# Eleven half chunks of second weights held back instead of fourteen, and five token tiles stored by halves of their rows instead of six

## The chip, the cores and the metric

One core of a Trainium2 chip runs the whole program. The metric is device time in microseconds (us) of one execution: the median of the runs before is 177.27 us, from 177.13 to 177.78 in three runs. The execution that the profiler recorded took 176.73 us, and its span, from the first recorded instruction to the last, is 175.0 us. Every time of the form "at 151.5" below counts from the start of that span.

## What is computed

Windowed attention over 8 batches, 8 heads, 576 positions and 64 features per head (one half of the heads with a plain window of 32, the other with a dilated one), then a soft mixture of 8 experts with 4 slots each over all 4608 tokens of 512 features.

```python
attn = softmax(mask(q @ k.T / sqrt(64))) @ v          # per batch and head
x = attn.transpose(0, 2, 1, 3).reshape(4608, 512)
logits = x @ phi                                      # 4608 x 32 slots
d = softmax(logits, axis=tokens)
slot_input = (d.T @ x).reshape(8, 4, 512)
for e in range(8):
    h = relu(slot_input[e] @ w1[e])                   # 512 -> 1024
    slot_out[e] = h @ w2[e]                           # 1024 -> 512
c = softmax(logits, axis=slots)
out = c @ slot_out                                    # 4608 x 512, float32
```

The part that the change touches is the end: the product with the second weights `w2` (8 experts of 1024 x 512), which gives 32 rows of 512, and the last line, which multiplies these 32 rows with every token's weights and stores 9.44 MB of output.

## The kernel before

The kernel is a list of operations with costs and due times. A planner (`Prog.schedule`) puts them in an order for each engine when the program is built, and `Prog.emit` writes that order out with the semaphore waits between engines. GpSimd and SyncE keep the order of the text. While the attention of 8 units runs, GpSimd issues every load: q, k and v of the units, then the first weights w1 of all experts, then the second weights w2. All loads are float32 in memory and become bfloat16 on the way in. They go through one queue, so they land in the order in which they were issued.

The second weights of one expert are 8 chunks (`cc` = 0 to 7), each 128 partitions by 512 columns. The load of an expert is one transfer, or several where `wload` gets a list of parts: (first chunk, last chunk, first column, last column). A piece of one chunk with 256 of its 512 columns is a half chunk here. The last three experts' second weights lie in the buffer `TT` (in the profile `TT<-in_moe_w_dram`, from line 496): w25 whole, then w26 (expert 6) and w27 (expert 7) in six transfers: two whole chunks of w26, the left column halves of its other six chunks, the left halves of w27 in two pieces, then the right halves of w26's six chunks, then the right halves of w27 in two pieces. So fourteen half chunks, all of right halves, come last: these are the ones held back.

The end of the kernel uses this order. `ffn2` multiplies hidden rows with chunks of w2, on four column groups of TensorE at once, into one PSUM bank, `sp_` (line 1017 in the profile). A call with `h_` None works on all 512 columns, with `h_` 0 or 1 on the left or right 256. When the left half of the columns is complete, `half(0, ...)` runs before the rest of the weights has come: VectorE scales the 32 rows into `so_sb` (line 1051), and for each of the first `NAB` token tiles (256 tokens each, two rows of the output to a partition) TensorE multiplies (lines 1069 and 1082), VectorE or ScalarE scales the result by the row sums `rtok` into a buffer in `WD` (lines 1051, 1052 and 1094), and the left halves of the rows are stored at once. Tile 0 is stored in two pieces of 128 KB, the others in one of 256 KB. Stores of even tiles are issued by SyncE (SP), those of odd tiles by ScalarE (ACT) on a queue of its own, both from line 1046. After the rest of the weights, `half(1, ...)` does the same with the right halves. The remaining tokens then go in larger groups (line 1126, tiles of 512 or 1024 tokens with whole rows): two groups of 4 rows to a partition, two of 8, each stored whole by SP, 1 MB, 1 MB, 2 MB and 2 MB.

A stored half row is 256 floats, 1024 bytes in one piece in memory; a whole row tile has 2, 4 or 8 rows in one piece to a partition, so 4, 8 or 16 KB.

Between waits TensorE runs products of a constant buffer (`filler`, line 1144), which the planner puts in where it expects a gap; nothing that they compute is used.

Names for what follows: `wload("w26", ...)` at lines 905 and 907, `NAB` and `GRP` at lines 979 and 980, the list of `ffn2` calls from line 1100, the last loop from line 1112.

Of the kernel before, what the change touches and what calls it, by code (L numbers as in the profile page):

```python
# [57 lines left out]
class Op:  # L58
    n = 0
# [58 lines left out]
class Prog:  # L118
# [6 lines left out]
    def op(self, e, fn, r=(), w=(), a=(), alloc=(), cost=0.5, key=0.0, mode="f",  # L125
           sem=None, nbytes=0, after=(), ndma=1, n=0, port=False):
        o = Op(e, fn, cost, key, mode)
        deps = list(after)
        for b in r:
            deps += b.ready  # L130
        for b in w:
            b.fresh()
            deps += b.prev
        for b in a:
            deps += b.prev
        seen = set()
        for d in deps:
            if d.id not in seen:
                seen.add(d.id)
                o.deps.append(d)  # L140
        for b in r:
            b.reads.append(o)
        for b in list(w) + list(a):
            b.ready.append(o)
        o.wr = [b for b in list(w) + list(a) if b.pool is not None]
        for b in list(r) + list(w) + list(a):
            if b.pool is not None and b not in o.touch:
                b.left += 1
                o.touch.append(b)
        o.alloc = list(alloc)  # L150
        o.sems = sem
        o.bytes = nbytes
        o.ndma = ndma
        o.n = 2 * n
        o.port = port
        self.ops.append(o)
        return o
# [171 lines left out]
def bass_dilated_sliding_attn__then__soft_moe_slots_kernel(  # L329
# [64 lines left out]
    def tile(pool, size=1):  # L394
        t = Buf(pool)
        t.size = size
        return t
# [8 lines left out]
    def pair(t):  # L406
        return ps[:, t.phys[0]:t.phys[0] + 2, :]

    def bank(t):
        return ps[:, t.phys[0], :]  # L410
# [68 lines left out]
    def wload(name, parts=((0, 8, 0, 512),)):  # L479
        ap, b = HOME[name]  # L480
        e = int(name[2:])
        first_ = name[:2] == "w1"
        src = (moe_w1 if first_ else moe_w2)[e]
        c = 4 if first_ else 8
        v_ = src.rearrange("(p c) f -> p c f", c=c)
        d_ = ap.rearrange("p (c f) -> p c f", c=c)
        for lo, hi, c0, c1 in parts:
            if first_:
                dst, vs = d_, v_
            else:  # L490
                dst, vs = d_[:, lo:hi, c0:c1], v_[:, lo:hi, c0:c1]
            sem = DmaSem(nc, f"s_{name}_{len(b.parts)}")
            pb = Buf()
            for al in b.al:
                pb.prev = pb.prev + al.ready + al.reads
            o = op("pool", lambda g, dst=dst, vs=vs: [g.dma_start(dst, vs)],  # L496
                   after=pb.prev, a=[pb], cost=0.6, sem=sem,
                   nbytes=2097152 * (hi - lo) * (c1 - c0) * (108 if c1 - c0 < 512 else 100) // 409600)
            b.parts.append((lo, hi, c0, c1, pb))
            b.ready.append(o)  # L500
# [401 lines left out]
                st_L(u - 1 + bpar, u)  # L902
    wload("w25")
    op("pool", lambda g: g.memset(hTT[:], 0.0), w=[b_scr] + b_hT + b_hT7, cost=1.2)
    wload("w26", ((0, 2, 0, 512), (2, 8, 0, 256)))
    wload("w27", ((0, 4, 0, 256), (4, 8, 0, 256)))
    wload("w26", ((2, 8, 256, 512),))
    wload("w27", ((0, 4, 256, 512), (4, 8, 256, 512)))

    K1 = 1000.0  # L910
# [26 lines left out]
    for hh in range(2):  # L937
        for y in range(2):
            def pe(t, hh=hh, y=y):
                for c in range(2 * y, 2 * y + 2):  # L940
                    for hi in range(2):
                        for j in range(4):
                            i_ = t.matmul(pair(hp)[32 * j:32 * j + 32, hh, :], siT[:, hi, c, j, :],
                                          w1v[j + 4 * hi][:, c, 512 * hh:512 * hh + 512],
                                          start=(c == 0 and hi == 0), stop=(c == 3 and hi == 1))
                return i_
# [29 lines left out]
            return en.activation(d_, s_, ACTF.Copy) if p_ == 0 else en.tensor_copy(d_, s_)  # L976
        op("act" if p_ == 0 else "dve", ev7, r=[ht], w=[b_hT7[p_]], cost=0.2, key=K1 + 1)

    NAB = 6
    GRP = [2] * NAB + [4, 4, 8, 8]  # L980
    rs = tile(psum, 1)
    COLS, d_ = [], 0
    for n in GRP:
        COLS += [(d_ + j, d_ + 128 * n, n) for j in range(n)]
# [19 lines left out]
    def ffn2(items, h_, key, after=()):  # L1004
        hs = (0, 1) if h_ is None else (h_,)
        sl = ALL if h_ is None else CH[h_]
        pbs = [pb for e, cc in items for l2, h2, c0, c1, pb in HOME[f"w2{e}"][1].parts
               if l2 <= cc < h2 and c0 < sl.stop and c1 > sl.start]

        def pe(t):  # L1010
            for e, cc in items:
                j, hi = e % 4, e // 4
                if e == 7:
                    j, l_ = cc % 4, hT7[:, cc, :]
                else:
                    l_ = hT[:, hi, cc, j, :]
                i_ = t.matmul(bank(sp_)[32 * j:32 * j + 32, sl],
                              l_, w2v[e][:, cc, sl],
                              start=(hi == 0 and cc == 0), stop=(e == 7 and cc >= 4),
                              skip_group_check=True)  # L1020
            return i_
        n = max(sum(1 for e, cc in items if (cc if e == 7 else e) % 4 == g) for g in range(4))
        o = op("pe", pe, r=list(dict.fromkeys(b_hT + b_hT7 + pbs)), alloc=[] if chain else [sp_],
               a=[sp_] + [b_sp[x] for x in hs], cost=(0.22 if h_ is None else 0.12) * n, mode="c",
               key=key, after=chain[-1:] + list(after))
        chain.append(o)
        for e in {e for e, _ in items}:
            HOME[f"w2{e}"][1].reads.append(o)
# [6 lines left out]
    def row(d0, n):  # L1035
        return [expT[:, d0 + j:d0 + 128 * n:n] for j in range(n)]
# [12 lines left out]
    def scaled(en, d_, s_, k_):  # L1049
        if en is nc.vector:  # L1050
            return en.tensor_scalar(d_, s_, k_, None, op0=AluOp.mult)  # L1051
        return en.activation(d_, s_, ACTF.Copy, scale=k_)  # L1052

    AB = [(256 * o, osts[o // 2][:, 1024 * (o % 2):1024 * (o % 2) + 1024].rearrange(
        "p (j f) -> p j f", j=2), b_ost[o // 2]) for o in range(NAB)]

    def half(h_, key):
# [4 lines left out]
           r=[b_sp[h_], b_rcs, sp_], w=[b_so[h_]], cost=0.45, key=key)  # L1062
        for o in range(NAB):
            d0, ap, prev = AB[o]
# [34 lines left out]

    ffn2([(e, cc) for cc in range(8) for e in range(4)], None, K1 + 2)  # L1100
    ffn2([(e, cc) for cc in range(2) for e in (4, 5, 6)], None, K1 + 3)
    ffn2([(e, cc) for cc in range(2, 8) for e in (4, 5)], None, K1 + 4)
    ffn2([(6, cc) for cc in range(2, 8)], 0, K1 + 10)
    ffn2([(7, cc) for cc in range(4)], 0, K1 + 11)
    ffn2([(7, cc) for cc in range(4, 8)], 0, K1 + 12)
    mm0 = half(0, K1 + 20)
    ffn2([(6, cc) for cc in range(2, 8)], 1, K1 + 30, after=mm0)
    ffn2([(7, cc) for cc in range(4)], 1, K1 + 31)
    ffn2([(7, cc) for cc in range(4, 8)], 1, K1 + 32)
    half(1, K1 + 40)  # L1110

    d0, n0 = 256 * NAB, 2 * NAB
    for i, (n, hs) in enumerate(((4, (3,)), (4, (4,)), (8, (5, 6)), (8, (7, 8)))):
        if hs[-1] == 8:
            ap = stg[:, 2, 0:8192].bitcast(F32)
        else:
            ap = WD[:, hs[0]:hs[-1] + 1, :].rearrange("p a x -> p (a x)").bitcast(F32)
        ap = ap.rearrange("p (j f) -> p j f", j=n)
        prev = [x for h in hs for x in b_ost[h]]
        ob = Buf()  # L1120
        for j0 in range(0, n, 2):
            po = tile(psum, 2)

            def pe(t, d0=d0, n=n, j0=j0, po=po):
                for j in range(2):
                    i_ = t.matmul(pair(po)[:, j, :], row(d0, n)[j0 + j], so_sb[:], start=True, stop=True)
                return i_
            key = K1 + 60 + 10 * i + j0
            op("pe", pe, r=b_so + b_expT, w=[po], alloc=[po], cost=0.45,
               key=key)  # L1130
            for j in range(2):
                op(("act", "dve")[j], lambda en, ap=ap, po=po, j=j, j0=j0, n0=n0: scaled(
                    en, ap[:, j0 + j, :], pair(po)[:, j, :], rtok[:, n0 + j0 + j:n0 + j0 + j + 1]),
                   r=[po, b_rtok], a=[ob], after=prev, cost=0.6, key=key)
        store(d0, n, ap, ob, K1 + 70 + 10 * i)
        d0 += 128 * n
        n0 += n
# [59 lines left out]
```

## Time and profile before

| what | value |
|---|---|
| median of 3 runs | 177.27 us (177.13 to 177.78) |
| the profiled execution | 176.73 us |
| its span | 175.0 us |
| TensorE matmul busy | 143.7 us, 82% of the span |
| VectorE busy | 111.8 us, 64% |
| ScalarE busy | 94.3 us, 54% |
| GpSimd busy | 65.9 us, 38% |
| read from memory, written to it | 61.93 MB, 9.44 MB |

Busy time of an engine is the time in which it had an instruction in work, as an average over the whole span. The stages differ: attention and the loads' first use fill the first 125 us or so, and from 164 us on no engine computes at all while the stores finish. The 16 DMA engines that move the data have a busy share of their own in each slice of the span, with the rate that they moved. For a load that halves its size on the way in, that rate counts the bfloat16 bytes written, not the float32 bytes read.

### The profile page before, as it was taken

How to read it: one execution, taken by the hardware profiler on the slowest of the kernel's cores; microseconds unless marked ns; L12 is line 12 of the kernel's file. 1: busy time of each engine (PE TensorE's matmuls, PEld its weight loads, DVE VectorE, ACT ScalarE, POOL GpSimd, SP SyncE). 2: the span in 40 equal slices, each digit the busy share in tenths (PEclk: the TensorE clock that was granted, in tenths of full speed). 3: DMA queues.
4: the chain of work that ended last, by engine and by line, in shares of the span. 5: the costliest groups of instructions: out<-in, count | busy, mean ns of one | idle time of the engine just before them, and what ended most of it. 6: DMA issues, size and time to landing. Idle time of an engine off the chain costs nothing.

```text
span 175.0 us, 5243 instructions
## 1 busy us (share of the span) xinstructions
PE 143.7 (82%) x2300; PEld 102.6 (59%) x2300; DVE 111.8 (64%) x257; ACT 94.3 (54%) x147; POOL 65.9 (38%) x111
## 2 busy tenths in 40 slices
PE   7699785998998898999989999779997898599000
PEld 2166564887696776797877798555664434343000
DVE  6830993289788999959989679994403002489300
ACT  2045835596984856798677979253021001589300
POOL 6983397103983105972002769498000000000000
PEclk9969999579999999999999999999999999969755
DMA  5999999999999999999999999999999999999997
GB/s 70 204 206 209 248 213 193 217 210 217 235 216 197 213 214 213 241 210 199 216 208 219 215 210 213 225 212 217 212 208 210 211 193 197 301 352 406 451 419 300
DMA packets 12550, 40.77 MB, mean 233 GB/s; under 512 B 2192, under 2 KB 8848, under 8 KB 8976
## 3 DMA queue, kind: packets, MB, share of 16 engines
q0 software_dynamic: 8128, 30.94, 88.3%
q1 hardware_dynamic: 2768, 7.93, 11.4%
q10 hardware_dynamic: 1632, 1.57, 2.6%
q8 instruction: 18, 0.29, 0.6%
q14 instruction: 4, 0.03, 0.0%
HBM read 61.93 MB, written 9.44 MB: 408 GB/s over the span
## 4 chain that ended last, share of the span: by engine, by line
PE 29%; DMA 28%; DVE 22%; POOL 8%; ACT 3%; issue 2%; POOLq 0%; DVEq 0%
DMA TT<-in_moe_w_dram 17%; DMA stg<-in_v_dram 11%; DVE XB L743 7%; PE ps L626 5%; DVE PT L693 4%; PE ps L678 4%; PE ps L703 4%; PE ps L760 3%; PE ps L632 3%; PE ps L787 3%; DVE VN L708 3%; POOL TT L496 2%; DVE WD L1051 2%; POOL stg L449 2%; PE ps L732 2%
## 5 line engine op out<-in xcount | busy, mean ns | idle before, releaser
L660 ACT ACTIVATE TT<-ps 128x864 f32<-128x864 f32 x32 | 28.0, 898 | 25.1 <-PE ps L632 17.5
L685 ACT ACTIVATE PT<-ps 128x768 bf16<-128x768 f32 x48 | 36.1, 815 | 5.4 <-PE ps L678 5.4
L743 DVE TENSOR_TENSOR XB<-ps,RV 96x768 bf16<-96x768 f32 x32 | 30.3, 947 | 0.5
L1144 PE MATMUL ps<-wrm 128*128 128x512 bf16 x74 | 22.5, 445 | 1.1 <-DVE wrm L513 1.1
L708 DVE COPY VN<-ps 128x768 bf16<-128x768 bf16 x32 | 17.2, 538 | 9.0 <-PE ps L703 9.0
L1052 ACT ACTIVATE WD<-ps,rtok 128x256 f32<-128x256 f32 (+1 forms) x22 | 10.5, 555 | 16.7 <-PE ps L1069 15.0
L632 PE MATMUL ps<-ident,stg 96*128 96x96 bf16 x288 | 15.5, 213 | 4.1 <-DMA stg<-in_v_dram 3.3
L732 PE MATMUL ps<-VN,PT 128*128 128x65 bf16 x384 | 17.0, 194 | 1.6 <-DVE PT L693 0.8
L678 PE MATMUL ps<-TT 64*128 64x96 bf16 x384 | 16.1, 211 | 2.2 <-DVE XT L772 0.6
L599 POOL COPY stg<-stg 96x576 f32<-96x576 f32 x24 | 17.0, 710 | 1.5
L703 PE MATMUL ps<-ident,TT 128*128 128x128 bf16 x192 | 17.2, 229 | 0.3
L632 PEld LDWEIGHTS ps<-ident,stg 96*128 96x128 bf16 x288 | 13.8, 102 | 5.8 <-DMA stg<-in_v_dram 4.0
L732 PEld LDWEIGHTS ps<-VN,PT 128*128 128x128 bf16 x384 | 14.2, 98 | 3.7 <-DVE XB L743 1.1
L678 PEld LDWEIGHTS ps<-TT 64*128 64x128 bf16 x384 | 10.1, 98 | 8.1 <-ACT PT L685 3.1
L773 ACT ACTIVATE XT<-ps 128x576 bf16<-128x576 bf16 x18 | 11.4, 652 | 5.0 <-PE ps L760 5.0
L693 DVE TENSOR_TENSOR PT<-PT,mask_d 128x768 bf16<-128x768 bf16 x24 | 14.0, 616 | 0.1
L1144 PEld LDWEIGHTS ps<-wrm 128*128 128x128 bf16 x74 | 7.5, 113 | 10.6 <-issue 6.0
L703 PEld LDWEIGHTS ps<-ident,TT 128*128 128x128 bf16 x192 | 11.8, 102 | 2.7 <-ACT TT L660 0.4
L449 POOL DMA_DIRECT2D stg<-in_q_dram x8 | 4.1, 521 | 24.3 <-PE ps L632 24.3
L693 DVE TENSOR_TENSOR PT<-PT,mask_p 128x768 bf16<-128x768 bf16 x24 | 12.4, 534 | 0.6 <-ACT PT L685 0.6
L760 PE MATMUL ps<-ident,XB 96*128 96x96 bf16 x192 | 11.7, 211 | 1.2 <-DVE XB L743 0.9
L626 PE MATMUL ps<-ident,stg 96*128 96x96 bf16 x216 | 11.1, 206 | 1.9 <-POOL stg L599 0.9
(98 smaller groups left out, 215.7 us busy)
## 6 DMA issues: line engine op xcount, KB each, us to landing
WD<-in_moe_w_dram POOLq DMA_DIRECT2D x7, 1024.0 KB, 25.1
stg<-in_moe_w_dram POOLq DMA_DIRECT2D x5, 1024.0 KB, 32.9
stg<-in_q_dram POOLq DMA_DIRECT2D x10, 288.0 KB, 20.6
stg<-in_k_dram POOLq DMA_DIRECT2D x10, 288.0 KB, 22.5
stg<-in_v_dram POOLq DMA_DIRECT2D x10, 288.0 KB, 24.1
out_dram<-WD SPq DMA_DIRECT2D x2, 1024.0 KB, 5.5
out_dram<-WD SPq DMA_DIRECT2D x1, 2048.0 KB, 8.7
out_dram<-stg SPq DMA_DIRECT2D x1, 2048.0 KB, 10.9
```

The costliest lines, as they stand in the source:

```text
L599: return g.tensor_copy(o_, i_)
L626: i_ = t.transpose(bankb2(pt, a)[:, 96 * kk:96 * kk + 96], il_ap(u, j, a)[:, 128 * kk:128 * kk + 128], ident[0:96, 0:96])
L632: i_ = t.transpose(bankb2(pt, a)[:, 96 * kk:96 * kk + 96], two[:, c, :], ident[0:96, 0:96])
L660: return ac.activation(d, sv, ACTF.Copy)
L678: i_ = t.matmul(pair(sc)[:, hx, QB * x:QB * x + QB], win(u, 1, h01, blk_, bpar)[64 * hx:64 * hx + 64], win(u, 0, h01, blk_, bpar)[64 * hx: ...
L685: op("act", lambda ac: ac.activation(sbt(pt)[:, 0:768].rearrange("p (x n) -> p x n", x=2), pair(sc)[:, :, 0:384], ACTF.Exp, scale=SCALE), ...
L693: return dv.tensor_tensor(p_, p_, m.unsqueeze(1).to_broadcast([128, 2, 384]), AluOp.mult)
L703: i_ = t.transpose(bankb(pv)[:, 128 * m:128 * m + 128], win(u, 2, h01, m, bpar), ident[:, :])
L708: op("dve", lambda dv: dv.tensor_copy(sbt(vn)[:, :, :, 0:64], bankb(pv)[:, 0:768].rearrange("p (m x d) -> p m x d", m=6, x=2)), r=[pv], w= ...
L732: i_ = t.matmul(pair(po)[:, bk, 65 * po_:65 * po_ + 65], sbt(pts[i])[:, o_:o_ + 128], sbt(vn)[:, m, half, 0:65], start=True, stop=True)
L743: op("dve", lambda dv: dv.tensor_tensor(sbt(xb)[:].rearrange("p m (x h d) -> p h x m d", x=2, h=2)[:, h01], pv()[:, :, :, 0:64], sbt(rv)[: ...
L1144: i_ = te.matmul(bank(t).rearrange("p (a x) -> p a x", a=4), wrm[:], wrm[:].unsqueeze(1).to_broadcast([128, 4, 128]), start=True, stop=True)
```

## The change

Three places move together. The load of w26 has five whole chunks in its first part instead of two, so three half chunks of each side remain (the held back ones are 3 + 4 + 4 = 11 instead of 6 + 4 + 4 = 14). The `ffn2` calls follow: chunks 2 to 4 of expert 6 are multiplied over all columns along with experts 4 and 5, and only chunks 5 to 7 by halves. And five token tiles are stored by halves instead of six; the sixth becomes a group of its own ahead of the four large ones, with whole rows, two to a partition, in the same place of `WD` (the last 1024 floats of its third slab), stored by SP as one transfer of 512 KB.

```diff
-    wload("w26", ((0, 2, 0, 512), (2, 8, 0, 256)))
+    wload("w26", ((0, 5, 0, 512), (5, 8, 0, 256)))
     wload("w27", ((0, 4, 0, 256), (4, 8, 0, 256)))
-    wload("w26", ((2, 8, 256, 512),))
+    wload("w26", ((5, 8, 256, 512),))
     wload("w27", ((0, 4, 256, 512), (4, 8, 256, 512)))
...
-    NAB = 6
-    GRP = [2] * NAB + [4, 4, 8, 8]
+    NAB = 5
+    GRP = [2] * NAB + [2, 4, 4, 8, 8]
...
-    ffn2([(e, cc) for cc in range(2, 8) for e in (4, 5)], None, K1 + 4)
-    ffn2([(6, cc) for cc in range(2, 8)], 0, K1 + 10)
+    ffn2([(e, cc) for cc in range(2, 8) for e in (4, 5, 6) if e < 6 or cc < 5], None, K1 + 4)
+    ffn2([(6, cc) for cc in range(5, 8)], 0, K1 + 10)
...
-    ffn2([(6, cc) for cc in range(2, 8)], 1, K1 + 30, after=mm0)
+    ffn2([(6, cc) for cc in range(5, 8)], 1, K1 + 30, after=mm0)
...
-    for i, (n, hs) in enumerate(((4, (3,)), (4, (4,)), (8, (5, 6)), (8, (7, 8)))):
+    for i, (n, hs) in enumerate(((2, (2,)), (4, (3,)), (4, (4,)), (8, (5, 6)), (8, (7, 8)))):
...
-        ap = ap.rearrange("p (j f) -> p j f", j=n)
+        ap = ap[:, ap.shape[1] - 512 * n:].rearrange("p (j f) -> p j f", j=n)
```

In the order that the planner makes of it, nothing moves on any engine ahead of the product with the second weights. There, TensorE has 27 filler products in place of 19 ahead of the first use of w26, and 5 in place of 2 and 4 between the pieces of the left half. The left and the right half each lose one pair of line 1082, two instructions of ScalarE (line 1052) and one store on ACT's queue; line 1126 gains one pair, line 1051 and line 1052 one eviction of 128 x 512 each, and SP one store.

## The prediction

> **What bounds the kernel now.** I read the slices of the page first, then the chain that ended last, then the stage from 147 us to the end: its DMA queues, its engines by the microsecond, its timeline.
>
> ```profile
> DMA  5999999999999999999999999999999999999997
> GB/s 70 204 206 209 248 213 193 217 210 217 235 216 197 213 214 213 241 210 199 216 208 219 215 210 213 225 212 217 212 208 210 211 193 197 301 352 406 451 419 300
> ```
>
> The DMA row is full from the second slice to the last: the transfers are the resource that never rests. The rate row counts what lands: about 200 GB/s while float32 becomes bfloat16, then stores at about 350 and at about 400 to 450. The chain says the same of the weights (3 of its 15 pieces):
>
> ```profile
> 119.41 1.52 POOL TT L496 x2
> 120.93 30.59 DMA TT<-in_moe_w_dram
> 151.52 0.04 issue
> ```
>
> It then runs through VectorE to its last eviction at 163.5, but that is the release of the last store, not what holds it: the store is issued at 163.63, its queue is busy with earlier ones until 169. So the sum has to be one of bytes and rates, plus every time in which a DMA engine has nothing to move. The stage where that could happen, by the microsecond (columns: busy PE, PEld, DVE, ACT, POOL, the clock, DMA share, GB/s):
>
> ```profile
> 149.00:150.00 1.00, 1.00 (x9) 0.50 (x6) 0.92 (x2) 0.66 (x2) 0.00 (x0) 1.00 1.46 200
> 150.00:151.00 1.00, 0.30 (x5) 0.10 (x4) 0.00 (x0) 0.84 (x2) 0.00 (x0) 1.00 1.19 320
> 151.00:152.00 1.00, 0.29 (x4) 0.10 (x4) 0.09 (x1) 0.35 (x1) 0.00 (x0) 1.00 1.06 360
> 152.00:153.00 1.00, 0.55 (x5) 0.51 (x6) 0.51 (x2) 0.35 (x2) 0.00 (x0) 1.00 1.01 344
> ```
>
> No microsecond between the last weights and the first stores is empty. (The share over 1 is that of transfers that overlap on one engine.) How close that is, the timeline shows:
>
> ```profile
> 146.88 0.29 PE L1017 MATMUL ps<-TT,hTT 128*32 128x256 bf16 x4
> ...
> 148.59 12.74 SPq L1046 DMA_DIRECT2D out_dram<-WD  x11
> ...
> 151.56 0.29 PE L1017 MATMUL ps<-TT,hTT 128*32 128x256 bf16 x4 [1.05 <-DMA TT<-in_moe_w_dram]
> ```
>
> The left half is complete at 146.88, the first store is issued at 148.59, and in the trace's list of packets its first one starts at 149.92: 3.04 us after 146.88. The held back weights are there to fill this time. A transfer is spread over 16 DMA engines, and the trace keeps 16 reports for each, which come some 0.35 us after the data. The last weights report at 150.28 first, twelve engines by 150.66, the slowest at 151.52. So twelve engines are out of weights at 149.9 to 150.3, just when the first store arrives, and the slowest four later. The reports of the last store lie at 174.34 to 174.54: by then all are level. So on the early engines the two edges meet with nothing to spare.
>
> **The change, part by part.** The profiled execution took 176.73 us for a span of 175.0, and its data ended at 174.19.
>
> (a) Three pairs of half chunks of w26 become three whole chunks. The rows are the reports of one engine: the six left halves of w26 took 1.96 us, 0.327 a piece; the two whole chunks before them 1.28 us, 0.64 a piece. Three pairs cost 1.96, three whole chunks 1.92. A longer stretch of whole chunks moved at 0.21 MB/us, 0.62 for a chunk of 0.131 MB, which makes it 1.86. Gain 0.04 to 0.1 us; I take 0.1.
>
> (b) The left half is complete later. Before it now come 5 whole chunks and 3 halves (5 x 0.63 + 3 x 0.33 = 4.14 us) where 2 and 6 came (1.28 + 1.96 = 3.24): 0.9 us later, so 146.88 becomes 147.8. TensorE's own part is hidden: it must wait for the five chunks in one, until about 144.05 in place of 142.2, and 8 rounds of column groups at 0.215 us (142.66, 142.87, 143.09 in the timeline) end at 145.8, ahead of the first piece of w27's left half at 146.4 (145.5 and 0.9). The five filler products behind that piece are queued ahead of the next: from 146.65 at 0.213 us (four took it from 145.77 to about 146.65) to 147.7, just done in time. If this cover is gone, it costs up to 0.2 us.
>
> (c) The first store follows at 149.92 + 0.9 = 150.8. The weights end as before less (a): 149.8 on the early engines, 151.1 on the slowest. So the twelve early engines, which hold 75% of the transfers, have nothing for about 0.6 to 1.0 us, and the slowest ones have no gap. This is the new wait, and what is late behind it is every store.
>
> (d) One tile of 512 KB leaves the half stores. Those move packets of 1024 bytes: 2.46 MB in the 7 us from 152 to 159, 0.352 MB/us. The big ones move at 0.42 (2.10 MB from 159.13 to 164.2, 4.19 MB from there to 174.19). The new one has 4096 bytes in a piece, which no row here has; by 1024-byte packets it would save nothing, by 8192-byte ones 0.524 x (1/0.352 - 1/0.42) = 0.24 us. I take 0.24, since a piece holds two whole rows and the row above is for four. The Trainium skill ("DMA: Bandwidth & Descriptors", Specifications) says that transfers of 512 bytes and more go at line rate. By it 1024-byte packets lose nothing and (d) would be 0; the trace disagrees, 45 ns for 1024 bytes and 313 for 8192, 22.8 against 26.2 bytes per ns. With the rule my sum would be 0.24 us higher.
>
> (e) Two instructions of ACT (0.42 each), one matmul pair and one store issue on ACT's queue (0.54 to 1.05) go from each half; one pair at line 1126, evictions of 0.74 (VectorE) and 0.58 (ScalarE) and one SP store are added behind. They cost nothing as long as data is ready before the queue runs dry. VectorE's first eviction of line 1126 began at 155.18 and takes 0.74, and ScalarE, with two fewer ahead, is done with its own by then: the whole tile is ready at about 155.9, and its data start 1.35 us after the issue (148.59 to 149.92), 157.3; the queue needs it at 158.3. The first group of four rows needs two more evictions of VectorE, ready at 157.4, with data from 158.8, needed at 159.5. If that cover goes, the excess counts in full. SP's queue is in order; behind the new store stand only the groups that are later anyway.
>
> The sum, by two bounds. If only bytes count and all engines stay full to the end, -0.1 - 0.24 = -0.34 us. If the early engines set the end: first store 150.8, 2.62 MB of half stores at 0.352 = 7.45, 0.52 + 6.29 MB at 0.42 = 16.2, end 174.5. The same sum for before is 149.92 + 8.94 + 14.98 = 173.84 where 173.97 (early) to 174.19 (late) was measured, so +0.65 on the early engines, which had 0.2 us to give. I take the second less that slack, +0.4, because three quarters of the engines are in that position and a transfer is done when its last share is. In the profiled execution's terms that is 177.1; the median of the runs is 0.54 above it, so 177.27 + 0.4 = 177.7.
>
> **The rivals.**
>
> A, the forecast: the early engines' gap outweighs the larger packets. 177.7, its own range 177.3 to 178.2. Chance 0.60.
>
> B, the gap is taken up: the stretch 152.0 to 152.5 already falls to 281 and 320 GB/s in its slices and still all engines end level, so some slack exists. Then the bytes count, -0.34: 176.9. Against it: the packet sum for before leaves at most 0.35 us of slack over the tail. Chance 0.18.
>
> C, clearly slower: the right half's first store comes after the left half's stores have run out. Five tiles last 1.31 / 0.352 = 3.7 us from 150.8, to 154.5; the right half's first data is due 3.04 us after 151.5, at 154.5. From that point each tenth later is a tenth at the end. What could make it later is ScalarE, whose left half now ends near 152.0 with 152.7 needed, or the clock, which falls to 0.50 after a thin stretch of TensorE (154 to 156 before). A miss of 0.6 us on top of A gives 178.3. For it: nothing is left between the two numbers. Against: ScalarE has less to do. Chance 0.17.
>
> D, a fixed cost per transfer: the change stores one tile in one transfer where it took two. A store of 256 KB lands 3.8 (ACT) to 4.3 us (SP) after its issue, of which its bytes at 0.352 MB/us are 0.75; if the other 3 us or so were paid one store after the other, one fewer would save 3 us: 174.3. The rows speak against it: the fourteen half stores, 3.15 MB, are through in 9.6 us (149.92 to 159.51), so their fixed costs lie beside each other. [...] Chance 0.02.
>
> E, the change does not do what it says: the early store is not on any path and the packets are alike; no change, 177.3. Chance 0.03.
>
> **How the numbers follow.** A measurement of this kernel tells about 0.5% from no change, 0.89 us: 176.4 to 178.2. Slower holds most of C and the upper end of A, 0.14 + 0.08 = 0.22. Faster holds D and the lower end of B, 0.04. The rest is 0.74. The range runs from B's 176.9 less a tenth to a little above C, 176.8 to 178.4; it leaves out D and a C with a larger miss.
>
> **What would show it.** The first left-half store's issue near 149.5 in place of 148.59, and the microsecond from 150 with a dip below 300 GB/s or a DMA share below 1: then (b) and (c) hold. A left half complete at 147.8 shows (b). The 512 KB store landing in about 1.25 us of queue time shows (d). No dip, with the first store at 150.8, makes B. A second dip near 154.5 makes C. The forecast is wrong if the end of data moves by more than the dip, or if it moves earlier.

## The result, and the profile after

The changed kernel is slower by 0.36%: its runs stand to those of before as 1.0036, 95% interval 1.0021 to 1.0052 (medians 178.00 us of 13 runs and 177.29 us of 13 runs). On 177.29 us that is 0.64 us, 0.37 to 0.92 (the ratio is taken over all runs; the two medians alone differ by 0.71). The ratios of this text leave out one run that was far slower than the others of its kernel, 247.29 us among the twelve of b_shortfill. The profiled execution of the changed kernel took 177.66 us with a span of 175.9, against 176.73 and 175.0.

The page of the changed kernel, the two rows of DMA slices and the queues of the stores:

```profile
DMA  4999999999999999999999999999999999899997
GB/s 69 205 212 218 242 205 191 219 215 208 245 203 204 216 213 217 230 205 205 219 209 218 214 212 222 212 218 212 222 203 214 209 195 195 238 342 414 456 421 298
...
q1 hardware_dynamic: 2912, 8.46, 12.2%
q10 hardware_dynamic: 1088, 1.05, 1.8%
```

Only one slice is no longer 9 that was 9 before, the 35th, which holds 149.5 to 153.9 us, and its rate fell from 301 to 238 GB/s. The slices behind it are much as they were. ACT's queue (q10) moves 1.05 MB in place of 1.57, SP's (q1) the rest: the tile has moved as the text says. The chain still starts with the weights, and they still land at the same time:

```profile
119.43 1.48 POOL TT L496 x2
120.91 30.57 DMA TT<-in_moe_w_dram
151.48 0.04 issue
```

So the loss lies behind the weights. The stage by the microsecond (columns as before: busy PE, PEld, DVE, ACT, POOL, the clock, DMA share, GB/s):

```profile
149.00:150.00 1.00, 1.00 (x11) 0.72 (x9) 0.84 (x2) 0.95 (x3) 0.00 (x0) 1.00 1.20 170
150.00:151.00 1.00, 0.54 (x7) 0.24 (x7) 0.88 (x2) 0.67 (x3) 0.00 (x0) 1.00 0.60 147
151.00:152.00 1.00, 0.29 (x4) 0.10 (x4) 0.13 (x1) 0.43 (x1) 0.00 (x0) 1.00 0.51 166
152.00:153.00 1.00, 0.59 (x6) 0.54 (x7) 0.51 (x2) 0.27 (x1) 0.00 (x0) 1.00 1.05 340
```

In the two microseconds from 150, the DMA engines are little more than half busy where they were full (1.19 and 1.06), and the rate is 147 and 166 GB/s in place of 320 and 360. From 152 on they are full again. This is the hole, and the timeline has its edges:

```profile
147.84 0.29 PE L1017 MATMUL ps<-TT,hTT 128*32 128x256 bf16 x4
...
149.55 11.51 SPq L1046 DMA_DIRECT2D out_dram<-WD  x12
...
151.52 0.29 PE L1017 MATMUL ps<-TT,hTT 128*32 128x256 bf16 x4 [0.99 <-DMA TT<-in_moe_w_dram]
```

The left half is complete at 147.84 instead of 146.88, the first store is issued at 149.55 instead of 148.59, and the right half is complete at 151.52 instead of 151.56.

A measure for what follows: the trace lists every packet with its start and length. Idle time is here the time in which fewer than 16 packets were in flight, each missing one counted as a sixteenth. From 149 to 152 us it is 0.00 in the trace of before and 0.96 us in that of the changed kernel; from 152 to 160 it is 0.10 and 0.05.

### The profile page after: what moved, and what is told of

Read it like the earlier page. It is cut to its first block, busy times and chain, and to the rows that moved or that the text cites. A ratio compares the mean times of both kernels' runs of the same rounds, so it can differ in the third digit from the quotient of the medians.

```text
span 175.9 us, 5244 instructions
## 1 busy us (share of the span) xinstructions
PE 140.8 (80%) x2302; PEld 101.4 (58%) x2302; DVE 112.3 (64%) x258; ACT 93.0 (53%) x144; POOL 65.3 (37%) x111
## 3 DMA queue, kind: packets, MB, share of 16 engines
q10 hardware_dynamic: 1088, 1.05, 1.8%
## 4 chain that ended last, share of the span: by engine, by line
DMA 28%; PE 28%; DVE 18%; POOL 8%; ACT 7%; issue 1%; POOLq 0%; DVEq 0%
DMA TT<-in_moe_w_dram 17%; DMA stg<-in_v_dram 11%; PE ps L626 5%; DVE XB L743 5%; PE ps L632 4%; PE ps L678 4%; PE ps L703 4%; ACT PT L685 4%; DVE WD L1051 3%; PE ps L760 3%; DVE PT L693 3%; PE ps L787 3%; POOL TT L496 2%; PE ps L732 2%; POOL stg L449 2%; DVE VN L708 2%
## 5 line engine op out<-in xcount | busy, mean ns | idle before, releaser
L1144 PE MATMUL ps<-wrm 128*128 128x512 bf16 x81 | 21.4, 403 | 1.1 <-DVE wrm L513 1.1
L1052 ACT ACTIVATE WD<-ps,rtok 128x256 f32<-128x256 f32 (+1 forms) x19 | 9.4, 583 | 17.3 <-PE ps L1069 16.7
L703 PE MATMUL ps<-ident,TT 128*128 128x128 bf16 x192 | 16.6, 223 | 0.7 <-ACT TT L660 0.2
L703 PEld LDWEIGHTS ps<-ident,TT 128*128 128x128 bf16 x192 | 11.3, 100 | 3.1 <-ACT TT L660 0.6
L741 DVE RECIPROCAL RV<-ps 96x12 f32<-96x12 f32 x32 | 7.1, 221 | 8.5 <-PE ps L732 8.4
```

Source lines behind the costliest of these rows:

```text
L703: i_ = t.transpose(bankb(pv)[:, 128 * m:128 * m + 128], win(u, 2, h01, m, bpar), ident[:, :])
L1144: i_ = te.matmul(bank(t).rearrange("p (a x) -> p a x", a=4), wrm[:], wrm[:].unsqueeze(1).to_broadcast([128, 4, 128]), start=True, stop=True)
```

## The experiments

The kernels ran in four groups, each on a chip of its own and with its own runs of the kernel before (medians 176.79 to 177.27 us), so ratios are compared and not medians across groups. All results, with the idle time of each kernel's trace in two stages:

| kernel | held back, tiles by halves | ratio to before (95% interval) | idle 149 to 152 | idle 152 to 157 |
|---|---|---|---|---|
| before, two traces | 14, 6 | 1 | 0.00, 0.14 | 0.07, 0.13 |
| the changed kernel, two traces | 11, 5 | 1.0036 (1.0021 to 1.0052) | 0.96, 1.11 | 0.03, 0.02 |
| w5_n6 | 11, 6 | 1.0059 (1.0046 to 1.0072) | 1.28 | 0.24 |
| w4_n6 | 12, 6 | 1.0018 (1.0003 to 1.0033) | 0.44 | 0.14 |
| w2_n5 | 14, 5 | 1.0016 (1.0008 to 1.0025) | 0.25 | 0.68 |
| w0_n6 | 16, 6 | 0.9996 (0.9987 to 1.0006) | 0.04 | 0.78 |
| w0_n7 | 16, 7 | 1.0001 (0.9992 to 1.0010) | 0.00 | 0.15 |
| a_whole0 | 11, 5, tile 0 whole | 1.0035 (1.0021 to 1.0049) | 1.25 | 0.05 |
| a_shortfill | 11, 5, all fillers short | 1.0084 (1.0056 to 1.0113) | 0.79 | 0.06 |
| b_shortfill | 14, 6, all fillers short | 1.0042 (1.0010 to 1.0074) | 0.01 | 0.02 |
| a_fetch146 | 11, 5, early fillers short | 1.0021 (1.0012 to 1.0030) | 0.85 | 0.06 |
| b_fetch146 | 14, 6, early fillers short | 0.9992 (0.9983 to 1.0000) | 0.14 | 0.04 |

An idle time is that of one execution, and executions of one kernel differ by 0.3 us and more, so the two kinds of columns agree only so far.

**Each part alone.** w5_n6 has the weights' part of the change, w2_n5 the tiles' part. (The `ffn2` calls and the last loop, left out here, follow as in the change itself.)

```diff
 w5_n6, against the changed kernel
-    NAB = 5
-    GRP = [2] * NAB + [2, 4, 4, 8, 8]
+    NAB = 6
+    GRP = [2] * NAB + [4, 4, 8, 8]
...
 w2_n5, against the changed kernel
-    wload("w26", ((0, 5, 0, 512), (5, 8, 0, 256)))
+    wload("w26", ((0, 2, 0, 512), (2, 8, 0, 256)))
...
-    wload("w26", ((5, 8, 256, 512),))
+    wload("w26", ((2, 8, 256, 512),))
...
```

> The weights' part of the change alone: eleven half chunks held back, six tiles by halves. Theory (lost cover): the DMA engines run out of weights before the first left-half store comes, about 1 us of idle time as a mean over 16 engines between 149.5 and 151.8, less 0.1 for the whole chunks: 0.9 slower than before, 178.2. Rival (the tile that left the half stores is the cause): no change, 177.2 to 177.3.

> The tiles' part alone: fourteen half chunks held back as before, five tiles by halves. Theory (lost cover, at another place): no hole at 150, but the left half's five tiles last 3.7 us from 149.9, to 153.6, and the right half's first data comes at 154.6, so a hole of some 0.7 to 0.9 us on the early engines ahead of 154.6, less 0.16 to 0.24 for larger packets: 177.6 to 177.9. Rival (only the weights' part costs): larger packets are won, 177.0 to 177.1.

w5_n6 came out 1.05 us slower (0.59%), as the theory of lost cover has it, and its rival is out: the weights' part makes the hole, with the old tiles too. In its trace, from 150 to 152 us:

```profile
150.00:151.00 1.00, 1.00 (x14) 0.71 (x13) 1.00 (x3) 1.00 (x4) 0.00 (x0) 1.00 0.34 53
151.00:152.00 1.00, 0.37 (x7) 0.09 (x1) 0.50 (x1) 0.65 (x3) 0.00 (x0) 1.00 0.47 136
```

TensorE, VectorE and ScalarE are all at full work in the first of these microseconds while the DMA engines have a third of theirs. w2_n5 came out 0.28 us slower, a little less than the 0.3 to 0.6 of the theory but on its side of no change, and its hole is where it was expected, between the last store of the left half and the first of the right half:

```profile
153.00:154.00 1.00, 1.00 (x10) 0.81 (x9) 0.74 (x2) 0.85 (x3) 0.00 (x0) 0.82 1.04 352
154.00:155.00 1.00, 1.00 (x4) 0.44 (x3) 0.95 (x2) 0.72 (x2) 0.00 (x0) 0.50 0.70 236
155.00:156.00 1.00, 1.00 (x4) 0.39 (x3) 0.84 (x2) 1.00 (x2) 0.00 (x0) 0.50 0.79 267
```

Alone the parts cost 1.05 and 0.28, together 0.64. They don't add up: with a hole at 150 the left half's stores come about 1 us later, and then five tiles last until the right half's first store. The changed kernel has no second hole (0.03 us idle from 152 to 157). What is left of the tiles' part is then its gain. By the medians this gain would be 0.41 (1.05 less 0.64), more than the 0.16 that its packets give below; the intervals are wide enough for both, and the rest is not explained.

**More cover, and less taken away.** w0_n7 and w0_n6 hold back all sixteen half chunks, with seven and with six tiles; w4_n6 holds back twelve, with six (whole chunks 0 to 3 of w26, then halves). w0_n6 sets `NAB` and `GRP` as w5_n6 does.

```diff
 w0_n6 and w0_n7, against the changed kernel
-    wload("w26", ((0, 5, 0, 512), (5, 8, 0, 256)))
+    wload("w26", ((0, 8, 0, 256),))
...
-    wload("w26", ((5, 8, 256, 512),))
+    wload("w26", ((0, 8, 256, 512),))
...
 w0_n7
-    NAB = 5
-    GRP = [2] * NAB + [2, 4, 4, 8, 8]
+    NAB = 7
+    GRP = [2] * NAB + [2, 4, 8, 8]
...
```

> The change the other way: all sixteen half chunks of the last two experts held back, seven tiles by halves, in the order 2 rows, 4, 8, 8 behind. Theory: nothing runs dry in before, so more cover wins nothing, and one more tile in small packets costs 0.16 to 0.24 and the half chunks 0.05: 177.5. Rival (before still has unfilled holes that cover would fill): faster, 177.0 or less.

> Sixteen half chunks held back, six tiles by halves. Theory: the left half is done 0.6 us earlier, its stores share the DMA engines with the last weights; the bytes are the same, but the left half's tiles may run out before the right half's come: 177.3 to 177.7. Rival (cover alone counts, more of it is better): faster than before, 177.0 or less.

> Twelve half chunks held back, six tiles by halves. Theory (lost cover): fourteen are just enough and each one less opens the hole by some 0.33 us, so 0.66 of hole less 0.07 for whole chunks: 177.8 to 177.9, between before and eleven with six tiles (178.26). Rival (a step: the hole opens only when the held issue of SP falls into it): 177.3 or 178.2, nothing between.

Neither of the first two is faster than before, and neither is slower: more cover wins nothing, since almost nothing was idle before (0.00 and 0.14 us from 149 to 152). For w0_n7 the expected loss of 0.2 us did not show either (0.02, -0.14 to 0.18), and w0_n6, at 177.17, lies a little below the 177.3 to 177.7 of its theory. w0_n6 has 0.78 us of idle time between 152 and 157 in its trace without a loss in its median; its profiled execution took 177.50, 0.33 above its median, and one trace can't tell whether the hole is in most executions. That stays open. w4_n6 lost 0.32 us (0.05 to 0.58), half of what was expected, though the value lies between before and w5_n6, as it must where the hole grows with the cover that is missing. The two half chunks from fourteen to twelve cost 0.32 together, the one from twelve to eleven 0.73. One half chunk is worth some 0.33 us of bytes, and the range of that second step, 0.38 to 1.08 by the two intervals together, just leaves it out. In w4_n6 two stores of SP were out before a long issue came (1.45 us at 149.97), in w5_n6 one (1.23 us at 150.56). Whether this makes the step was not tested with these two kernels; the next experiments look at the long issue in the changed kernel.

**The held store.** In the changed kernel SP's second store takes long to issue. First before, its fourth store, then the changed kernel, its second (start, duration in us):

```profile
150.12 1.51 SPq L1046 DMA_DIRECT2D out_dram<-WD  x1
```

```profile
149.94 1.25 SPq L1046 DMA_DIRECT2D out_dram<-WD  x1
```

Others of the same size take 0.43 (half of tile 0, the second store of before) or 0.61 us (a tile, the third store of before). Length alone is no sign of a common cause, though: in the changed kernel SP also needs 1.27 us at 156.20 and 1.15 at 158.40, with many stores ahead in the queues. Before, 768 KB of stores had been issued at 150.12, on both queues, and no idle time followed. In the changed kernel only the first 128 KB had. By its packets, its data run from 150.40 to about 151.0 on most engines; ScalarE's first store has its first packet at 151.56, and the held one at 152.24. So both kernels were traced a second time, and tile 0 was stored whole.

```diff
 a_whole0, against the changed kernel
+                ob0 = Buf()
                 for j in range(2):
...
-                    ob = Buf()
+                    ob = ob0
...
-                    store(d0, 2, ap, ob, k2, h_, j)
+                store(d0, 2, ap, ob, k2, h_)
```

> The kernel before once more, for a second trace: how much of its first trace's empty tail (0.1 us of idle DMA time from 149 to 160) is that one execution, which was 0.5 us below the median. Theory: a typical execution has some 0.2 to 0.5 us of idle time there. Rival: always near 0.1.

> The changed kernel once more, for a second trace. Theory: the hole of 1 us between 149.5 and 151.8 is there in every execution, with the second store of SP held at its issue for over 1.2 us. Rival: the held issue belongs to one execution and the hole is 0.6 to 0.75 without it.

> The changed kernel with tile 0 stored by SP as one half store of 256 KB in place of two of 128 KB. Theory (part of the hole is the second piece, held at its issue): the first store carries 0.74 us of data at once, idle time 0.7 in place of 0.96: 177.7 to 177.8. Rival (only the start of the first data counts): it starts up to 0.1 us later, and the same hole stands behind it: 178.0 to 178.1.

The second trace of before has 0.30 us of idle time from 149 to 160, the first 0.10; that of the changed kernel 1.15 and 1.01, with the second store held for 1.32 us. So hole and hold come back. a_whole0 did not help: 1.0035 beside 1.0036, with 1.25 us of idle time where its theory had 0.7. Its first store is issued in 0.61 us at 150.23, but its first packet starts at 151.48, 1.25 us after the issue instead of 0.85. The hole only moved. By the idle time the theory is out. The rival has the loss, but not the start of the data, which it put at most 0.1 us later: it was 1.1 us later, half of it because the left half itself was complete only at 148.40 in this trace. By the time alone (1.0021 to 1.0049) the two can't be told apart.

In these traces, and in those of all the kernels above, a packet of 16 KB on the instruction queue (q8) starts at 149.9 to 150.6, when TensorE has had 2303 to 2307 weight loads, whatever else was changed. That this packet belongs to TensorE's program is read from this count. Two pairs of kernels move this point by the number of TensorE's instructions ahead of it. The filler products are made as two of 256 columns each, all of them or only those that the planner puts into the first 20 us (`at` is the planned time):

```diff
 a_fetch146 and b_fetch146; a_shortfill and b_shortfill have m = 2 throughout
-            for _ in range(n):
-                i_ = te.matmul(bank(t).rearrange("p (a x) -> p a x", a=4), wrm[:],
-                               wrm[:].unsqueeze(1).to_broadcast([128, 4, 128]), start=True, stop=True)
+            m = 2 if at < 20.0 else 4
+            for _ in range(4 * n // m):
+                i_ = te.matmul(bank(t)[:, 0:128 * m].rearrange("p (a x) -> p a x", a=m), wrm[:],
+                               wrm[:].unsqueeze(1).to_broadcast([128, m, 128]), start=True, stop=True)
```

> The changed kernel with every filler product of 512 columns made as two of 256: the same filler time, 82 more weight loads and products in TensorE's program. In all ten traces so far one 16 KB packet on the instruction queue starts at 149.9 to 150.6, when TensorE is at its 2303rd to 2306th weight load, and in nine of them a store that SP issues within 0.5 us of it takes 0.8 to 1.6 us to issue in place of 0.43 to 0.61. Theory (the code fetch of TensorE holds the store): the fetch moves 82 weight loads earlier, SP's second store issues in 0.43, the hole falls from about 1.0 to 0.7 of idle time: 177.4 to 177.5 beside 177.8 for the changed kernel, both where before is 177.1 to 177.2. Rival (SP is held by the state of the DMA queues at that moment): the second store is held for 1.2 us as ever, no change against the changed kernel.

> The kernel before with the same edit to the filler. Theory (code fetch): no store of SP or ScalarE is held at 150, but nothing was missing there either, so the same time as before within 0.2 us; another store may be held where the next fetch falls, near 154.5, with data in the queue. Rival (state of the DMA queues): the fourth store is held for 1.5 us as ever. If doubling the fillers costs TensorE's own time, both kernels of this call are slower by the same amount.

> The changed kernel with only the 26 filler products of the first 20 us made as two of 256 columns each, so that TensorE's code fetch of about 150 comes 26 weight loads earlier, near 146, and, it is hoped, none at 165. Theory (the fetch at 150 holds SP's second store): the second store issues in 0.43 us, idle time in the hole 0.7 to 0.8, and the changed kernel's loss against before falls from 0.36% to 0.15 to 0.25%. Rival: the hold is not the fetch's, or the hole costs the same without it: loss of 0.36% as ever.

> The kernel before with the same edit. Theory: its fourth store is no longer held for 1.5 us, its tail was full anyway, so no change, within 0.1% of before. Rival: a fetch at 146 delays the weights on one DMA engine and costs 0.3 to 0.9 us, in both kernels of this call.

With all fillers short, the packet moved to 141.0 and 140.5, and the hold at 150 went. But both kernels became slower, and their runs spread wide (177.28 to 179.48 for a_shortfill). A new packet of 16 KB had come at 165.3 (164.7 in b_shortfill), among the last stores. From 160 us on, in a_shortfill:

```profile
q8 instruction: 1, 0.02, 0.3%
...
out_dram<-stg SPq DMA_DIRECT2D x1, 2048.0 KB, 13.5
```

and in the changed kernel:

```profile
out_dram<-stg SPq DMA_DIRECT2D x1, 2048.0 KB, 12.1
```

The last store lands 1.4 us later after its issue. By the sixteen reports of that store, fifteen engines had it at 175.44 (changed kernel 175.46), the last at 177.09 (175.48): one engine came 1.7 us late, and the store with it. In b_shortfill one engine of sixteen was late in the same way, 176.17 beside 174.30. So these two don't test the hold by their time, only by their trace.

a_fetch146 and b_fetch146 have no such late packet: theirs lie at 148.1 and 146.2. In a_fetch146 SP's second store is issued at once:

```profile
150.15 0.43 SPq L1046 DMA_DIRECT2D out_dram<-WD  x1
```

and the same stage then reads

```profile
150.00:151.00 1.00, 0.74 (x9) 0.31 (x7) 1.00 (x2) 0.82 (x3) 0.00 (x0) 1.00 0.63 149
151.00:152.00 1.00, 0.27 (x4) 0.10 (x4) 0.09 (x1) 0.47 (x1) 0.00 (x0) 1.00 0.68 216
```

The second microsecond moved 216 GB/s in place of 166. In finer slices, the rates from 149 to 155 us (0.15 us each) of the changed kernel, then of a_fetch146:

```profile
GB/s 198 201 171 167 143 198 68 58 44 198 314 260 75 41 55 34 21 273 341 355 335 335 321 362 348 342 328 355 362 314 335 375 348 348 335 328 362 355 314 341
```

```profile
GB/s 188 198 178 184 120 82 65 55 51 44 96 352 314 130 311 352 205 55 109 335 362 362 362 321 321 287 382 348 355 348 348 341 348 335 342 335 362 335 335 355
```

The long gap from 150.8 to 151.55 (75 down to 21) becomes two short ones around 151.0 and 151.7. But the stream is steady no sooner, and most of the hole is still there: idle time is 0.85 us, beside 0.96 and 1.11. The loss against before fell from 0.64 (0.37 to 0.92) to 0.37 us (0.21 to 0.53); the intervals overlap. b_fetch146, its counterpart, came out 0.14 us faster than before (0.00 to 0.30), though nothing had been missing there, so part of that step may be something else that the edit does. Against its counterpart a_fetch146 loses 0.51 us (0.37 less -0.14). What the hold costs is then 0.1 us (0.64 less 0.51) to 0.3 us (0.64 less 0.37), and not clear of nothing.

In four kernels out of four where the packet was moved, the long issue at 150 went: to 0.43 us for the second store of both a kernels, and to 0.83 for the fourth store of both b kernels, b_fetch146 here:

```profile
150.38 0.83 SPq L1046 DMA_DIRECT2D out_dram<-WD  x1
```

That the packet and the hold go together is shown by this; how the one holds the other is not, nor why 0.83 is left and not 0.61. b_fetch146 is also the best version that was found, 0.08% faster than before, at the edge of what its 11 runs can tell.

## Why the prediction was right, point by point

The prediction was 177.7 us with a range of 176.8 to 178.4 and "within 0.5%" as the likeliest; 178.0 and +0.36% were measured. Rival A happened; its 0.4 lies within the measured 0.37 to 0.92. The signs that the prediction named came too: the first store's issue at 149.55, the left half complete at 147.84, and the microsecond from 150 at 147 GB/s with a DMA share of 0.60.

(a) Whole chunks in place of halves, a gain of 0.1: the weights' last report moved from 151.52 to 151.48, 0.04 earlier, and the second pair of traces has 151.76 and 151.52. The sign held; a size of this kind is within what two executions differ by.

(b) The left half 0.9 us later: 0.96 (146.88 to 147.84). The product of the five chunks starts at 144.09 where 144.05 was forecast, and the five fillers end just as the last piece lands (its last report is at 147.78), so TensorE's part was hidden as said.

(c) This step gave the main term, and it is the one that was mis-sized. It left the twelve early engines without work for 0.6 to 1.0 us, 0.45 to 0.75 as a mean over sixteen; idle time was 0.96 and 1.11 us. Three things in it were off:

- The first packet came at 150.40, not 150.8. From the issue to the first packet it took 0.85 us; the 1.33 that the prediction carried over was that of one trace, and the second trace of before has 0.87.
- But it came alone. The prediction let a steady stream begin with the first packet; the first store is only 128 KB, and the stream was steady at about 151.6. The held second store, which the prediction had in its own rows (SP's fourth store before, 1.5 us long) and did not price, is a part of this. It is not all: without the hold a_fetch146 is steady no sooner, and its idle time is 0.85.
- The weights ended earlier than (a) allowed. The mean of their sixteen last reports is 150.31 and 150.22 in the two traces of the changed kernel, 150.63 and 150.49 in those of before: 0.3 earlier, where 0.1 was taken. The slowest engine, on which the semaphore waits, hardly moved. In the kernel before, the first stores share the DMA engines with the last weights, and in the changed kernel the early engines have little else to move; that this is the reason was not tested.

So the forecast was right by its mechanism, but its 0.4 owes something to luck: the first packet was put too late, and the stream behind it too early.

(d) Larger packets: 0.24 was taken. The new tile's packets of 4096 bytes take 164 ns, those of 1024 bytes 46, so its 32 KB on each engine take 8 x 164 = 1.31 us in place of 32 x 46 = 1.47: a gain of 0.16. The rule of the Trainium skill that 512 bytes and more go at line rate ("DMA: Bandwidth & Descriptors", Specifications) is not borne out by it: 22.3, 25.0 and, for 8192 bytes in 314 ns, 26.1 bytes per ns.

(e) The rest is hidden: from 152 to 160 no more idle time than before. The whole tile is issued at 156.20 and its data start at 158.80, directly behind the half stores.

The sum with measured sizes: mean idle time from 149 to 160 of 1.08 us (two traces) less that of before, 0.20, less 0.16 and 0.04, gives +0.68 beside the +0.64 of the runs. That close an agreement is partly luck: the same sum gives 0.37 for w4_n6 (0.32 measured), but 1.33 for w5_n6 (1.05) and 0.59 for w2_n5 (0.28), so it is good to some 0.3 us.

Rival B, in which the hole is taken up by slack, is out: the hole of about 1 us is there, and the kernel is slower by more than 0.37 us where B had it faster. Rival C, a second hole ahead of the right half, did not come in the changed kernel, but w2_n5 shows that it is real: it needs the early left half that the weights' part takes away. Rival D is out with the sign, and E, no change, with the interval.

## What to carry to other kernels

These come from one kernel. Where the DMA engines are full to the end, a transfer issued early is worth what it keeps busy, and work that is held back to bridge a latency should be counted in time on the engines that run out first, not on the slowest one that the semaphore waits for. Two cuts that each open a hole may not add up, when the first hole moves the stream past the second: measure them alone and together. And a bridge that is just long enough has to last until the new stream is steady, not until its first packet: look at how much the first transfer carries, and at issues that are long but harmless today.

## What the runs showed of the hardware

TensorE's place in its program set when a 16 KB packet came on the instruction queue, and two things went with that packet. Near its start, an SP store took 1.2 to 1.6 us to issue in place of 0.43 to 0.61 (eight of the nine traces of kernels with the old fillers and tile 0 in two pieces; 0.81 in the ninth, w0_n6; a_whole0 showed no long issue). In four of the eight, ScalarE's store beside it was long too, 1.05 to 1.13 us in place of 0.54 or 0.55. And where one fell among the last large stores, one DMA engine of sixteen came 1.7 to 1.9 us late (both short-filler kernels). The Trainium skill ("Runtime: NRT & Kernel Launch", Instruction fetch mechanics) says that instruction memory is refilled in blocks of 16 KiB, 256 instructions, over a DMA queue of the sequencer's own, and that the cost is mostly hidden. The traces agree on the 16 KB; hidden it was not, here: a store whose issue took 0.8 us longer in the changed kernel, and a last store landing 1.4 us later in a_shortfill.

The sixteen engines were not level: the last piece of weights was reported 1.2 us later by the slowest engine than by the fastest (150.28 and 151.52), and the last store 0.2 us later (174.34 and 174.54).
